# The gate of a noisy top-2 MoE kernel: its products accumulate in PSUM by quarters of a step and VectorE turns them, with no selection product

## The chip, the cores and the metric

The kernel runs on one core of a Trainium2 chip, in one launch, in fp32 and fp32r with a few bf16 tables. The metric is device time in microseconds. Three runs of the kernel before gave 718.95, 720.71 and 718.71 us, a median of 718.95 us.

## The reference, cut to what matters

A block-wise linear attention writes 3072 tokens of 512 features, and a mixture of 8 experts with a noisy top-2 gate follows on these tokens:

```python
# attention, per block of 64: out = ((q k^T) * Dmask) v + (q * lam_pow) kv_state
x = attn_out.transpose(0, 2, 1, 3).reshape(B * S, H * D)        # 3072 x 512
logits = x @ w_gate                                             # 512 x 8
noise_scale = np.log1p(np.exp(x @ w_noise))                     # 512 x 8
noisy_logits = logits + noise_scale * noise
top2 = np.argpartition(-noisy_logits, 2, axis=1)[:, :2]
# softmax over the two, then per expert e and choice k:
h = np.maximum(x[mask] @ w1[e], 0.0)
out[mask] += top2_w[mask, k, None] * (h @ w2[e])
```

The change concerns the two small products of the gate, `x @ w_gate` and `x @ w_noise`: 16 numbers per token out of 512 features.

## The kernel before, in words

**Two stages.** The first stage is the attention with the gate in it, up to about 140 us; the second is the experts. The order of every engine is written out by hand: the program is one long list, and each engine runs its own instructions in the order in which the list issues them.

**A step of the attention.** A step u is 256 tokens of all heads, two chunks `a` of 128; there are 12 steps. The loop `for t in range(NST)` (from L980) works on three steps at once. In iteration t TensorE turns the keys of step u = t + 1 (`trans_k`, L328), forms its key-value sums (`kv`, L419), turns its queries (`trans_q`, L344), does the product with the values of step t (`intra` and `inter`, L384), turns the output of step t - 1 into token rows (`store_x`, L450), does the gate's products of step t - 1 (`products`, L438), the scores of step u (`scores`, L372) and half of `inter`, and then the gate's selection of step t - 1 (`logits`, L466).

**The gate's products.** `wgn` holds gate and noise weights side by side, 16 columns and 16 zeros, for each of four blocks `d` of 128 features. `products` runs four matmuls, one per `d`, each over the 256 tokens of the step, into four groups of 32 partitions of the PSUM tile `pR`: the four partial sums stand below one another. ScalarE copies them to SBUF as `xp` (L440). `logits` multiplies `xp`, 128 tokens at a time, with the 0/1 matrix `sel` (made once by VectorE in `make_sel`, L256 to L259). This adds the four partial sums and puts the tokens on the partitions, into the PSUM tile `pL`. Each fp32 matmul stands in the trace as two records.

**PSUM tiles that are shared.** `pR` is one buffer, used in turn by `products`, by the second half of `kv` (a = 1) and by others. `pS` has four buffers: in an iteration `scores` takes all four, VectorE frees them with the masked copy `at` (L375, four instructions), and the next `trans_k` (three buffers) and `kv` (one) take them again.

**The routing.** The tokens are routed in three groups of 8 chunks (`GB`). After a group's last logits, VectorE runs `gate` (some 60 small instructions, beginning with a copy of the logits out of PSUM, L476), counts, and lists of tokens per expert tile. These jobs are Python generators; `advance(n)` issues about n us worth of them at two places of each iteration: after `trans_q` (`FILLS`, 3.4) and at its end (`FILL`, 2.0). A job that yields without a number counts 0.21. GpSimd computes the two softmax weights of a group, and `store_w` (L550) writes them with one DMA into the token rows in DRAM, on SP's queue.

**The end of the attention.** In the last iteration TensorE also turns the first gathered token rows (`trans_rows`, L874). Behind the loop come the first expert's first products (`mm1`, L895), the last step's products, `store_w(1)`, the last `store_x`, and the remaining list jobs. Then the attention's SBUF pools are closed, and the hidden tile `ht` takes their place: its first write, the ReLU of L901 on ScalarE, waits until all that used that memory is done, the DMA of the last `store_x` (L454) out of `xc` among it. VectorE's L905 forms the low part of `ht` and frees the PSUM buffer. The order of SP's queue there is: six DMAs of zeros into the output (L965), `store_w(1)`, the two of `store_x`, seventeen of zeros.

**Places.** A list entry is a token number, made by the one-hot matmuls of `enlist` from two parts, a chunk and a row in it (`tokb`, `rowf`, L621 to L648).

Of the kernel before, what the change touches and what calls it, by code (L numbers as in the profile page):

```python
# [59 lines left out]
HOT = 2 * (128 + NTL + NV * NTL)  # L60
NST = NCH // 2
NW = NC // 2
MAXOV = 40
ARENA = 1304
MAXT = 24
OPUS = 0.21
FILL, SPLIT, FILLS = 2.0, 1.2, 3.4
# [25 lines left out]
def sub(ap, offset, dims):  # L93
    return bass.AP(tensor=ap.tensor, offset=ap.offset + offset, ap=dims)
# [31 lines left out]
def kernel(  # L126
# [90 lines left out]
    def mask(s, h, c):  # L217
# [22 lines left out]
    iotar = consts.tile([128, TS], BF, name="iotar")  # L240
    nc.gpsimd.iota(iotar, pattern=[[1, TS]], base=0, channel_multiplier=0, allow_small_or_imprecise_dtypes=True)
    rowf = consts.tile([128, 1], FT, name="rowf")
    nc.gpsimd.iota(rowf, pattern=[[0, 1]], base=-TS, channel_multiplier=1, allow_small_or_imprecise_dtypes=True)
    tokb = consts.tile([128, NCH, NV], BF, name="tokb")
    nc.gpsimd.iota(tokb[:, :, 0], pattern=[[1, NCH]], base=-(BIG // TS), channel_multiplier=0,
                   allow_small_or_imprecise_dtypes=True)
    nc.gpsimd.iota(tokb[:, :, 1], pattern=[[0, NCH]], base=-TS, channel_multiplier=1,
                   allow_small_or_imprecise_dtypes=True)
    destf = consts.tile([128, 2, NCH], FT, name="destf")
    recs = consts.tile([128, NTL], I32, name="recs")  # L250
    sel = consts.tile([128, 2 * E], FT, name="sel")

    def make_sel():

        v = nc.vector
        v.tensor_scalar(sel, jp[:, 0:2 * E], 0.0, None, op0=OP.is_equal)  # L256
        for q in range(1, DB):
            v.tensor_scalar(sq4, jp[:, 0:2 * E], float(-32 * q), None, op0=OP.is_equal)
            v.tensor_add(sel, sel, sq4)  # L259

    sq4 = ac.tile([128, 2 * E], FT, name="sq4")

    class Arena:

        def __init__(self, n):
# [13 lines left out]
            return v  # L279

    arena = Arena(ARENA)
    for s, w in ((0, w_gate), (1, w_noise)):
        for d in range(2):
            for h in range(2):
                nc.gpsimd.dma_start(wgn[h * 64:(h + 1) * 64, d::2, s * E:(s + 1) * E],
                                  sub(w, (d * 128 + (h ^ d) * 64) * E, [[E, 64], [256 * E, DB // 2], [1, E]]))
# [29 lines left out]
    def half(i):  # L316
        return slice(i * 64, (i + 1) * 64)
# [115 lines left out]

    def products(u):

        p = psum.tile([128, 2, C], FT, name="pR")
        for d in range(DB):
            nc.tensor.matmul(p[d * 32:(d + 1) * 32], wgn[:, d, :], XO[u][:, :, d, :], start=True, stop=True)  # L438
        XP[u] = aw.tile([128, 2, C], FT, name="xp", bufs=1)
        nc.scalar.activation(XP[u], p, AF.Copy)  # L440

    XC = [ac.tile([128, DB, QW], FT, name=f"xc{i}") for i in range(3)]
    xturn = itertools.count()
# [12 lines left out]
    def logits(u):  # L456
        nonlocal pl
        for a in range(2):
            g = 2 * u + a
            b = max(i for i in range(NG) if GB[i] <= g)  # L460
            if not g:
                pl = psum.tile([128, 512], FT, name="pL")
            if g == GB[b]:
                PL[b] = pl[:, NV * NTL:][:, :GM * 2 * E].rearrange("p (c e) -> p c e", e=2 * E)
                PC[b] = pl[:, NV * NTL + GM * 2 * E:]
            nc.tensor.matmul(PL[b][:, g - GB[b], :], XP[u][:, a, :], sel, start=True, stop=True)  # L466


    def gate(b):
# [1 line left out]
        gs = GB[b + 1] - GB[b]  # L471
        sh = [128, gs, E]
        t = lambda sh, nm, dt=FT: arena.tile(sh, dt, name=nm)
        pl = PL[b]
        l2 = t([128, gs, 16], "l2")
        v.tensor_copy(l2, pl[:, :gs, :])  # L476
        yield
        zc = t(sh, "zc")
        v.tensor_scalar(zc, l2[:, :, 8:16], 87.0, -87.0, op0=OP.min, op1=OP.max)
        yield  # L480
# [65 lines left out]
        r["w"] = wd[:, 0]  # L546

    def store_w(b):
        rows = x_tok[GB[b] * C:GB[b + 1] * C, :].rearrange("(c p) w -> p c w", p=128)
        nc.sync.dma_start(rows[:, :, WAT:], RT[b].pop("w"))  # L550

    def count(b):
        gs = GB[b + 1] - GB[b]
# [63 lines left out]
    def loads(b, c, n, buf):  # L617

        _, hi, mv = hot(buf, n)
        mv = mv.rearrange("p k (w j) -> p k w j", w=NV)  # L620
        nc.vector.tensor_scalar(mv[:, :, 1, :], hi, rowf, None, op0=MULT)  # L621
        for i in range(n):
            k = slice(2 * i, 2 * i + 2)
            nc.vector.tensor_scalar(mv[:, k, 0, :], hi[:, k, :], float(GB[b] + c + i - BIG // TS), None, op0=MULT)

    found = consts.tile([128, NV, NTL], FT, name="found")

# [15 lines left out]
    def decode(s, out, n):  # L643

        v = nc.vector
        idf = rp.tile([128, n], FT, name=f"idf{n > 1}")
        v.scalar_tensor_tensor(idf, s[:, 0], float(TS), s[:, 1], op0=MULT, op1=ADD)
        v.tensor_scalar(out, idf, float(BIG + TS), None, op0=ADD)  # L648

    def read_lists(a, b):  # L650
# [31 lines left out]
        nc.vector.tensor_add(xo, xo, PO[0][0][half(g), g::2, :])  # L682
    kv(1)
    state(1)
    make_sel()
    inter(1, 1)

    def places(b):
# [292 lines left out]
    for t in range(NST):  # L981
# [16 lines left out]
        if not t:  # L998
            pass
        elif u < NST:  # L1000
            advance(FILLS)
        else:
            store_x(t - 1)
            products(t - 1)
            for j in range(PARTS0[0]):
                trans_rows(0, j)
            logits(t - 1)
            advance(FILLS)
        if t:
            intra(t)  # L1010
# [29 lines left out]
        if t >= NST - 2:  # L1040
            zero_out(3)
        if t == 2:
            nc.sync.dma_start(nz, sub(noise, 0, [[E, 128], [128 * E, NCH], [1, E]]))
    assert got
    finish(1)
    head = [mm1(0, 0, PARTS0[0], 0)]
# [280 lines left out]
```

## Time and profile before

| | |
|---|---|
| median of three runs | 718.95 us |
| span of the profiled execution, first to last instruction | 716.8 us |
| TensorE busy | 698.8 us, 97% |
| VectorE busy | 398.3 us, 56% |
| ScalarE busy | 223.3 us, 31% |
| GpSimd busy | 361.8 us, 50% |
| mean granted TensorE clock | 0.994 of full speed |
| largest share of the chain that ended last | TensorE, 89% |

The table says that TensorE is the engine to look at, and that it has hardly any idle time. It does not say what a microsecond taken from TensorE in one stage is worth: VectorE's 56% is a mean, and in the attention, where the gate's jobs run beside the masks, its share is far higher. So the stage of the change has to be read by itself, step by step. The profiled execution's own time is taken as its span; the median lies 2.15 us above it.

### The profile page before, as it was taken

The page shows a single profiled execution, that of the slowest core. Times are in us where ns is not written, and L with a number is a line of the kernel's source. Part 1 is how long each engine was busy: PE and PEld are TensorE (multiplying, and loading weights), DVE is VectorE, ACT ScalarE, POOL GpSimd, SP SyncE. Part 2 cuts the span into 40 slices and gives each one's busy share as a digit, 9 for nine tenths or more (in the row PEclk, how much of TensorE's full clock was granted, in tenths as well). Part 3 has the DMA queues.
Part 4 walks back from the last instruction along what each step waited for, and adds up shares of the span by engine and source line. Part 5 has one row for each costly group of instructions (what it writes and reads, how often), then busy time and mean ns, then how long its engine had stood idle before and what let it go on. Part 6 is the DMA issues. An engine that isn't in the chain of part 4 may idle for free.

```text
span 716.8 us, 15851 instructions
## 1 busy us (share of the span) xinstructions
PE 698.8 (97%) x6014; PEld 600.4 (84%) x6014; DVE 398.3 (56%) x1044; ACT 223.3 (31%) x382; POOL 361.8 (50%) x505
## 2 busy tenths in 40 slices
PE   7899999999999999999999999999999999999994
PEld 5888888889898898988888888888888898888883
DVE  4755899879355546743674367337624662565210
ACT  2255545542143312332233214222322242223100
POOL 4411342313453865687768567836773768321221
PEclk9999999999999999999999999999999999999998
DMA  9998986580645725273627352735452554330110
GB/s 203 263 230 245 251 232 203 188 305 25 180 131 168 207 56 179 82 185 87 183 93 176 85 186 84 176 88 161 116 154 79 170 143 122 104 116 30 51 51 32
DMA packets 94192, 104.32 MB, mean 146 GB/s; under 512 B 41234, under 2 KB 66844, under 8 KB 94112
## 3 DMA queue, kind: packets, MB, share of 16 engines
q1 hardware_dynamic: 79456, 65.73, 34.0%
q0 software_dynamic: 13552, 37.00, 17.0%
q10 hardware_dynamic: 1104, 0.53, 0.5%
q8 instruction: 49, 0.80, 0.5%
q14 instruction: 31, 0.25, 0.1%
HBM read 78.28 MB, written 26.12 MB: 146 GB/s over the span
## 4 chain that ended last, share of the span: by engine, by line
PE 89%; issue 4%; DMA 2%; POOL 1%; DVE 1%; ACTq 0%; SPq 0%; ACT 0%; POOLq 0%
PE pS L895 37%; PE pKV L933 16%; PE pO L933 16%; PE pO L384 3%; PE pS L372 3%; PE pS L328 2%; PE pS L450 2%; PE pO L938 2%; PE pS L419 2%; PE pS L344 1%; PE pKV L384 1%; PE pKV L938 1%; DMA Mk<-powd 1%; PE pR L438 1%; PE pS L874 1%
## 5 line engine op out<-in xcount | busy, mean ns | idle before, releaser
L839 POOL DMA_INDIRECT xg<-x_tok,recq x147 | 161.0, 1095 | 45.6 <-issue 40.0
L895 PE MATMUL pS<-xth,w1h 128*128 128x512 f32 (+3 forms) x544 | 181.4, 333 | 0.9 <-DVE ht L905 0.9
L895 PE MATMUL pS<-xth,w1l 128*128 128x512 f32 (+3 forms) x544 | 180.5, 332 | 0.0
L895 PE MATMUL pS<-xtl,w1h 128*128 128x512 f32 (+3 forms) x544 | 180.5, 332 | 0.0
L905 DVE SCALAR_TENSOR_TENSOR ht<-pS,ht 128x256 fp32r<-128x256 f32 (+3 forms) x176 | 75.8, 454 | 123.1 <-ACT ht L901 120.7
L933 PE MATMUL pKV<-w2h,ht 128*128 128x512 f32 x384 | 122.6, 390 | 0.0
L933 PE MATMUL pO<-w2h,ht 128*128 128x512 f32 x384 | 122.4, 390 | 0.0
L952 POOL DMA_INDIRECT out_dram<-ot,rec x46 | 60.7, 1319 | 121.0 <-DVE ot L945 110.8
L901 ACT ACTIVATE ht<-pS 128x512 fp32r<-128x512 f32 (+3 forms) x136 | 65.2, 483 | 173.2 <-PE pS L895 167.7
L895 PEld LDWEIGHTS pS<-xth,w1h 128*128 128x128 f32 x544 | 102.7, 189 | 10.4 <-DVE ht L905 1.1
L895 PEld LDWEIGHTS pS<-xth,w1l 128*128 128x128 f32 x544 | 102.7, 189 | 8.8
L895 PEld LDWEIGHTS pS<-xtl,w1h 128*128 128x128 f32 x544 | 102.7, 189 | 8.8
L933 PEld LDWEIGHTS pO<-w2h,ht 128*128 128x128 f32 x384 | 72.1, 188 | 14.9
L933 PEld LDWEIGHTS pKV<-w2h,ht 128*128 128x128 f32 x384 | 72.1, 188 | 14.9
L866 ACT ACTIVATE xth<-turned 128x512 fp32r<-128x512 f32 (+1 forms) x39 | 23.7, 607 | 167.5 <-DVE turned L864 167.5
L933 PE MATMUL pKV<-w2l,ht 128*128 128x512 f32 x192 | 74.9, 390 | 0.0
L933 PE MATMUL pO<-w2l,ht 128*128 128x512 f32 x192 | 74.8, 390 | 0.0
L360 POOL TENSOR_TENSOR kd<-kt,Mk 128x512 f32<-128x512 f32 x24 | 24.8, 1051 | 73.4 <-PE pR L419 51.6
L917 POOL DMA_INDIRECT pv<-out_dram,rec x46 | 47.0, 1021 | 14.2 <-issue 12.0
L375 DVE TENSOR_TENSOR at<-pS,Mk 128x512 f32<-128x512 f32 x48 | 29.9, 683 | 23.0 <-PE pS L372 18.5
L808 DVE TENSOR_TENSOR w2l<-wst,w2h 128x1024 fp32r<-128x1024 f32 (+1 forms) x33 | 39.2, 1191 | 6.1 <-ACT w2h L807 5.6
L933 PEld LDWEIGHTS pKV<-w2l,ht 128*128 128x128 f32 x192 | 36.1, 188 | 7.4
(241 smaller groups left out, 941.5 us busy)
## 6 DMA issues: line engine op xcount, KB each, us to landing
wst<-in_moe_w_dram SPq DMA_DIRECT2D x36, 512.0 KB, 4.2
wst<-in_moe_w_dram SPq DMA_DIRECT2D x96, 128.0 KB, 3.7
x_tok<-xc SPq DMA_DIRECT2D x24, 272.0 KB, 4.7
kt<-in_k_dram SPq DMA_DIRECT2D x12, 512.0 KB, 5.2
qt<-in_q_dram SPq DMA_DIRECT2D x24, 256.0 KB, 5.2
vt<-in_v_dram SPq DMA_DIRECT2D x12, 512.0 KB, 5.7
out_dram<-zero SPq DMA_DIRECT2D x24, 256.0 KB, 3.6
xg<-x_tok,recq POOLq DMA_INDIRECT x147, 2.8
```

Of the source, the lines that this page charges most:

```text
L360: nc.gpsimd.tensor_mul(kd[:, :, s], kt[:, :, s], mask(s, slice(0, HP), slice(C - 1, C)).to_broadcast([128, HP, 2, D]))
L375: nc.vector.tensor_mul(at[:, s], ps[s], mask(s, slice(2 * r, 2 * r + 2), slice(0, C)))
L384: nc.tensor.matmul(PO[u][a][half(g), hp, :], lhs, rhs, start=n == 1, stop=n == (8 if not (u % NW or a) else 12 if u else 10))
L808: nc.vector.tensor_tensor(lo[:, r], st[:, r], hi[:, r].bitcast(FT), op=SUB)
L839: nc.gpsimd.indirect_dma_start(out=XG[t][:, g * QW:(g + 1) * QW], out_offset=None, in_=x_tok.rearrange("t (q w) -> (t q) w", w=QW), in_off ...
L866: nc.scalar.activation(hi, raw, AF.Copy)
L895: nc.tensor.matmul(p, W1[a][d][:, fs], xt(b, cs)[:, d], start=(d == 0 and i == 0), stop=(d == DB - 1 and i == 2))
L901: nc.scalar.activation(ht(e, 0, f, cs), p, AF.Relu)
L905: nc.vector.scalar_tensor_tensor(ht(e, 1, f, c), p[:, r], 0.0, ht(e, 0, f, c).bitcast(FT), op0=OP.max, op1=SUB)
L917: nc.gpsimd.indirect_dma_start(out=PV[t][:size(e, t), :], out_offset=None, in_=out, in_offset=bass.IndirectOffsetOnAxis(ap=REC[e, t], axis=0),
L933: nc.tensor.matmul(p, ht(e, a, f, cs), W2[b][f // 2][:, f % 2, :], start=(i == 0), stop=(i == len(terms) - 1))
L952: st = nc.gpsimd.indirect_dma_start(out=out, out_offset=bass.IndirectOffsetOnAxis(ap=REC[e, t], axis=0), in_=o, in_offset=None, bounds_che ...
```

## The change

The products go by quarters of 64 tokens. For each block `d` of features and each quarter `j` there is one matmul of 64 columns, into the group `j` of 32 partitions of `pR`, and the four blocks `d` add up there in PSUM (`start` on the first, `stop` on the last). So 16 matmuls stand where 4 were, with as many columns in all. VectorE then turns the 128 x 64 tile in blocks of 32 x 32 straight out of PSUM (`transpose`), which puts the tokens on the partitions. ScalarE's copy `xp`, the two selection matmuls of a step, `sel` with `make_sel`, and the copy at the head of `gate` are gone. `pR` is now held until VectorE has turned it.

A token now stands on another partition: token 64 j + 32 g + i of a step is on partition 32 j + i, in column group g. So the noise and the weights are moved by eight DMAs each instead of one (128 descriptors of 32 bytes each for the weights), the place tables are built from more pieces, and the decoding of list entries uses 32 instead of 128. In the last iteration `logits` stands ahead of `trans_rows`, with one dummy matmul behind (`keep_warm(1)`).

```diff
-ARENA = 1304
+ARENA = 1432
-    nc.gpsimd.iota(rowf, pattern=[[0, 1]], base=-TS, channel_multiplier=1, allow_small_or_imprecise_dtypes=True)
-    nc.gpsimd.iota(tokb[:, :, 0], pattern=[[1, NCH]], base=-(BIG // TS), channel_multiplier=0,
...
+    for j in range(4):
+        for o, n in ((rowf, 1), (tokb[:, :, 1], NCH)):
+            nc.gpsimd.iota(o[j * 32:(j + 1) * 32], pattern=[[0, n]], base=64 * j - TS, channel_multiplier=1,
...
-        p = psum.tile([128, 2, C], FT, name="pR")
+        p = XP[u] = psum.tile([128, 2, 32], FT, name="pR")
         for d in range(DB):
-            nc.tensor.matmul(p[d * 32:(d + 1) * 32], wgn[:, d, :], XO[u][:, :, d, :], start=True, stop=True)
-        XP[u] = aw.tile([128, 2, C], FT, name="xp", bufs=1)
-        nc.scalar.activation(XP[u], p, AF.Copy)
+            for j in range(4):
+                nc.tensor.matmul(p[j * 32:(j + 1) * 32], wgn[:, d, :], XO[u][:, j // 2, d, half(j % 2)],
+                                 start=d == 0, stop=d == DB - 1)
...
-                PL[b] = pl[:, NV * NTL:][:, :GM * 2 * E].rearrange("p (c e) -> p c e", e=2 * E)
-                PC[b] = pl[:, NV * NTL + GM * 2 * E:]
-            nc.tensor.matmul(PL[b][:, g - GB[b], :], XP[u][:, a, :], sel, start=True, stop=True)
+                PL[b] = lg1 if b == 1 else arena.tile([128, GM, 32], FT, name="l2")
+                PC[b] = pl[:, NV * NTL:]
+            if not a:
+                nc.vector.transpose(PL[b][:, g - GB[b]:][:, :2, :].rearrange("p g e -> p (g e)"),
+                                    XP[u].rearrange("p g r -> p (g r)"))
...
-        l2 = t([128, gs, 16], "l2")
-        v.tensor_copy(l2, pl[:, :gs, :])
-        yield
+        l2 = PL[b][:, :gs, :]
...
-        rows = x_tok[GB[b] * C:GB[b + 1] * C, :].rearrange("(c p) w -> p c w", p=128)
-        nc.sync.dma_start(rows[:, :, WAT:], RT[b].pop("w"))
+        w = RT[b].pop("w")
+        for j in range(4):
+            for g in range(2):
+                rows = x_tok[GB[b] * C + 64 * j + 32 * g:, :]
+                nc.sync.dma_start(sub(rows, WAT, [[XW, 32], [2 * C * XW, w.shape[1] // 2], [1, E]]),
+                                  w[j * 32:(j + 1) * 32, g::2, :])
...
-    make_sel()
...
             products(t - 1)
+            logits(t - 1)
             for j in range(PARTS0[0]):
                 trans_rows(0, j)
-            logits(t - 1)
+            keep_warm(1)
             advance(FILLS)
...
-            nc.sync.dma_start(nz, sub(noise, 0, [[E, 128], [128 * E, NCH], [1, E]]))
+            for j in range(4):
+                for g in range(2):
+                    nc.sync.dma_start(nz[j * 32:(j + 1) * 32, g::2, :],
+                                      sub(noise, (64 * j + 32 * g) * E, [[E, 32], [2 * C * E, NST], [1, E]]))
```

TensorE's order in iteration 4, from `store_x` to the next `trans_k` (`xo` is the attention's output of a step, `qTs` the scaled queries, `S` a state; `pO` and `pKV` take the output). Before:

```order
L450 MATMUL pS<-identf,xo 128x128 x8
L438 MATMUL pR<-xo,wgn 32x256 x4
L372 MATMUL pS<-qT,kT 64x128 x32
L384 MATMUL pKV<-qTs,S_150 64x128
L384 MATMUL pO<-qTs,S_149 64x128
...
L466 MATMUL pL<-sel,xp 128x16 x2
L328 MATMUL pS<-identf,kt 128x128 x12
```

With the change:

```order
L441 MATMUL pS<-identf,xo 128x128 x8
L430 MATMUL pR<-xo,wgn 32x64 x16
L363 MATMUL pS<-qT,kT 64x128 x32
L375 MATMUL pKV<-qTs,S_150 64x128
L375 MATMUL pO<-qTs,S_149 64x128
...
L319 MATMUL pS<-identf,kt 128x128 x12
```

The selection is gone, so `trans_k` follows on `inter`, and the products have four times as many matmuls of a quarter of the columns.

VectorE's order from the masked copy of iteration 4 to that of iteration 5, where the first group's gate begins (`arena` is the gate's scratch memory; L476 is the copy out of PSUM; the constants' lines L101 to L118 are a polynomial). Before:

```order
L375 TENSOR_TENSOR at<-pS,Mk 128x512 x4
L476 COPY arena<-pL 128x128
L479 TENSOR_SCALAR arena<-arena 128x64
...
L500 TENSOR_TENSOR arena<-arena 128x64
L505 MAX arena<-arena 128x8
L375 TENSOR_TENSOR at<-pS,Mk 128x512 x4
L505 MAX arena<-arena 128x8 x7
```

With the change (`lg` takes the second group's logits):

```order
L366 TENSOR_TENSOR at<-pS,Mk 128x512 x4
L458 STREAM_TRANSPOSE arena<-pR 128x64
L469 TENSOR_SCALAR arena<-arena 128x64
...
L490 TENSOR_TENSOR arena<-arena 128x64
L495 MAX arena<-arena 128x8 x3
L366 TENSOR_TENSOR at<-pS,Mk 128x512 x4
L458 STREAM_TRANSPOSE lg_173<-pR 128x64
L495 MAX arena<-arena 128x8 x5
```

The transpose has the place of the copy, it comes in every iteration and not once a group, and two more instructions of the gate (L495) now stand ahead of the masked copy.

SP's order at the end of the attention, around `store_w(1)`. Before:

```order
L965 DMA out_dram<-zero 128x512 x3
L550 DMA x_tok<-arena 128x8x8
L454 DMA x_tok<-xc_183 128x544
L454 DMA x_tok<-xc_184 128x544
L965 DMA out_dram<-zero 128x512 x17
```

With the change:

```order
L959 DMA out_dram<-zero 128x512 x3
L543 DMA x_tok<-arena 32x4x8 x8
L445 DMA x_tok<-xc_188 128x544
L445 DMA x_tok<-xc_189 128x544
L959 DMA out_dram<-zero 128x512 x17
```

The last two stores of token rows now stand behind eight DMAs of weights instead of one.

## Rows read from the trace of the kernel before

**Rows 1.** The page's first line.

```profile
span 716.8 us, 15851 instructions
```

**Rows 2.** Busy time by stretch: PE, PEld, DVE, ACT, POOL, then clock, DMA share, GB/s.

```profile
108.00:126.00 18.00, 17.96 (x404) 15.23 (x402) 16.42 (x58) 10.11 (x19) 4.27 (x4) 1.00 0.65 200
```

**Rows 3.** Chain that ended last, attention: start us, us, engine, tile, line, records.

```profile
67.03 0.57 PE pR L438 x8
67.60 1.91 PE pS L372 x64
69.94 0.55 PE pL L466 x4
70.49 1.36 PE pS L328 x12
...
77.90 1.91 PE pS L372 x64
...
80.78 1.36 PE pS L328 x12
...
83.28 1.02 PE pS L344 x8
...
92.89 1.08 PE pS L419 x32
...
109.40 1.91 PE pS L372 x64
...
120.26 1.91 PE pS L372 x64
...
123.19 1.85 PE pS L328 x12
```

**Rows 4.** Timeline of PE: start us, us, engine, line, operation, out<-in, count.

```profile
91.19 0.34 PE L561 MATMUL pL<-arena,ones 128*128 128x8 bf16 x8
```

**Rows 5.** Timeline of DVE, iterations 4, 5, 8 and 9.

```profile
68.67 2.48 DVE L375 TENSOR_TENSOR at<-pS,Mk 128x512 f32<-128x512 f32 x4 [3.43 <-PE pS L372]
71.07 0.28 DVE L476 COPY arena<-pL 128x128 f32<-128x128 f32 x1
...
79.55 2.46 DVE L375 TENSOR_TENSOR at<-pS,Mk 128x512 f32<-128x512 f32 x4
81.93 0.56 DVE L505 MAX8 arena<-arena 128x8 f32<-128x8 f32 x7
...
110.47 2.48 DVE L375 TENSOR_TENSOR at<-pS,Mk 128x512 f32<-128x512 f32 x4 [0.72 <-PE pS L372]
...
122.46 2.46 DVE L375 TENSOR_TENSOR at<-pS,Mk 128x512 f32<-128x512 f32 x4
```

**Rows 6.** Line L864, VectorE's transposes later on: ns min/median/max, then forms.

```profile
L864 DVE STREAM_TRANSPOSE turned<-xg x39: 298/702/712, 268.1 to 641.6; 128x512 f32<-128x512 f32 x36, 128x128 f32<-128x128 f32 x3
```

**Rows 7.** Timeline of SP's queue at the end of the attention.

```profile
141.97 0.38 SPq L550 DMA_DIRECT2D x_tok<-arena  x1
143.09 1.05 SPq L454 DMA_DIRECT2D x_tok<-xc  x2
144.19 11.35 SPq L965 DMA_DIRECT2D out_dram<-zero  x17
```

**Rows 8.** Timeline of ACT and PE there.

```profile
146.31 0.66 ACT L901 ACTIVATE ht<-pS 128x256 fp32r<-128x256 f32 x2 [2.76 <-DMA x_tok<-xc]
...
146.85 1.58 ACT L807 ACTIVATE w2h<-wst 128x1024 fp32r<-128x1024 f32 x2
...
148.99 0.39 PE L895 MATMUL pS<-xth,w1h 128*128 128x256 f32 x1 [0.92 <-DVE ht L905]
```

**Rows 9.** Timeline of DVE there.

```profile
148.51 0.76 DVE L905 SCALAR_TENSOR_TENSOR ht<-pS,ht 128x256 fp32r<-128x256 f32 x2
149.18 1.81 DVE L808 TENSOR_TENSOR w2l<-wst,w2h 128x1024 fp32r<-128x1024 f32 x2
150.91 0.42 DVE L905 SCALAR_TENSOR_TENSOR ht<-pS,ht 128x256 fp32r<-128x256 f32 x1
```

More of the change, by code (lines that the diff above doesn't have):

```diff
@@ L62 @@
 NW = NC // 2
+QT32 = 32
 MAXOV = 40
-ARENA = 1304
+ARENA = 1432
 MAXT = 24
@@ L242 @@
     rowf = consts.tile([128, 1], FT, name="rowf")
-    nc.gpsimd.iota(rowf, pattern=[[0, 1]], base=-TS, channel_multiplier=1, allow_small_or_imprecise_dtypes=True)
     tokb = consts.tile([128, NCH, NV], BF, name="tokb")
-    nc.gpsimd.iota(tokb[:, :, 0], pattern=[[1, NCH]], base=-(BIG // TS), channel_multiplier=0,
-                   allow_small_or_imprecise_dtypes=True)
-    nc.gpsimd.iota(tokb[:, :, 1], pattern=[[0, NCH]], base=-TS, channel_multiplier=1,
-                   allow_small_or_imprecise_dtypes=True)
+    nc.gpsimd.iota(tokb[:, :, 0].rearrange("p (u g) -> p u g", g=2), pattern=[[8, NST], [1, 2]], base=-(BIG // QT32),
+                   channel_multiplier=0, allow_small_or_imprecise_dtypes=True)
+    for j in range(4):
+        for o, n in ((rowf, 1), (tokb[:, :, 1], NCH)):
+            nc.gpsimd.iota(o[j * 32:(j + 1) * 32], pattern=[[0, n]], base=64 * j - TS, channel_multiplier=1,
+                           allow_small_or_imprecise_dtypes=True)
     destf = consts.tile([128, 2, NCH], FT, name="destf")
     recs = consts.tile([128, NTL], I32, name="recs")
[L251 to L261, printed above, removed]
     class Arena:
@@ L281 @@
     arena = Arena(ARENA)
+    lg1 = ac.tile([128, GM, 32], FT, name="lg1")
     for s, w in ((0, w_gate), (1, w_noise)):
@@ L473, in gate @@
         t = lambda sh, nm, dt=FT: arena.tile(sh, dt, name=nm)
-        pl = PL[b]
-        l2 = t([128, gs, 16], "l2")
-        v.tensor_copy(l2, pl[:, :gs, :])
-        yield
+        l2 = PL[b][:, :gs, :]
         zc = t(sh, "zc")
@@ L623, in loads @@
             k = slice(2 * i, 2 * i + 2)
-            nc.vector.tensor_scalar(mv[:, k, 0, :], hi[:, k, :], float(GB[b] + c + i - BIG // TS), None, op0=MULT)
+            nc.vector.tensor_scalar(mv[:, k, 0, :], hi[:, k, :], float((GB[b] + c + i) // 2 * 8 + (c + i) % 2 - BIG // QT32), None,
+                                    op0=MULT)
     found = consts.tile([128, NV, NTL], FT, name="found")
@@ L646, in decode @@
         idf = rp.tile([128, n], FT, name=f"idf{n > 1}")
-        v.scalar_tensor_tensor(idf, s[:, 0], float(TS), s[:, 1], op0=MULT, op1=ADD)
+        v.scalar_tensor_tensor(idf, s[:, 0], float(QT32), s[:, 1], op0=MULT, op1=ADD)
         v.tensor_scalar(out, idf, float(BIG + TS), None, op0=ADD)
```

## The prediction

> **What bounds the kernel now.** I read the page first, then the busy time by stretch, the chain of waits over the attention, and the timelines of VectorE, SP and ScalarE where that chain leaves TensorE. The sum is made against the span of the profiled execution, 716.8 us [rows 1]; the median of the runs, 718.95 us, lies 2.15 above it, and I add the same 2.15 at the end. In the attention TensorE is busy 17.96 of 18 us at a granted clock of 1.00, but VectorE is not idle there either: 16.42 of 18 [rows 2]. So TensorE sets the pace with VectorE close behind. A step, from one scores group to the next, takes 77.90 - 67.60 = 10.30 us [rows 3]. The gate has two pieces in it: the products (L438, 0.57 us) and the selection (L466, 0.55 us), both on the chain [rows 3].
>
> **The selection's end.** Its 0.55 us do not all go. A full-array transpose costs 1.36 / 12 = 0.113 us (L328 behind the selection); L344 behind 64x64 work takes 1.02 for eight, where 8 x 0.113 would be 0.91 [rows 3]. The change of tile shape thus costs 0.11. The selection pays it today, as the first full-array work behind `inter`; with it gone `trans_k` pays it. Gain: 0.55 - 0.11 = 0.44 us a step.
>
> **The products.** They go from 8 records to 32, with the same columns. The scores are 64 records of 128 columns over four 64x64 tiles that run beside each other: 16 records a tile in 1.91 us, 0.119 each, 0.93 ns a column [rows 3]. Today a group of 32 partitions has 2 records of 256 columns, 0.48 us of 0.57; changed, 8 of 64 columns, again 0.48. What 24 more records cost is shown by `kv`: its full form, 64 records, runs from 80.78 + 1.36 = 82.14 to 83.28, 1.14 us; its half form, 32 records on two of the four tiles, takes 1.08 [rows 3]. 32 more records beside the others: 0.06 us. I take 0 for the products. From below the bound is 0.48 (-0.09 a step). From above, the tiny full-array matmuls of the counting run one behind the other, eight in 0.34 us, 0.043 each [rows 4]; 32 of these are 1.36 us (+0.79 a step). I stay with `kv`, which has small tiles, short records and PSUM accumulation too.
>
> One rule speaks against that. The Trainium skill, in "TensorEngine Tiling (Array Packing)", section "Instruction Overhead", gives every matmul some 60 cycles of overhead and advises against making a dimension smaller that is already small. By an estimate from this page, 24 more records at 25 ns would be 0.6 us a step, and the time 721.6 us; the `kv` pair above measures a tenth of that, so the trace does not agree where tiles run side by side, and I keep it as a reason for the second rival.
>
> **VectorE's transpose.** 128 x 64 out of PSUM stands nowhere in the trace. VectorE's transposes from SBUF take 0.298 us for 128 columns and 0.70 for 512 [rows 6], 1.05 ns a column, so 0.23 for 64; the copy of 128 x 128 out of PSUM, 0.28 [rows 5], bounds it from above, though a source in PSUM could add to that. I take 0.25. It stands behind the fourth masked copy and holds `pR` until its end; queued behind it are the gate's jobs, and who waits is the second half of `kv`. Where the masked copy is on time it starts 68.67 - 67.60 = 1.07 us after the scores and ends at 1.07 + 2.48 = 3.55, the transpose at 3.80 [rows 3, 5]. `kv` will be reached at 1.91 + 0.43 (`inter`) + 0.11 + 1.36 = 3.81. That just fits: no wait in iterations 1, 2, 3, 6 and 7, a gain of 5 x 0.44 = 2.20 us.
>
> **Where VectorE is late, the gain is lost.** In iterations 5 and 9 the masked copy starts with no idle time before it [rows 5]: VectorE comes straight from the gate's polynomials. Then TensorE's saved time only makes it wait longer for `pS` and `pR`.
>
> Iterations 4 and 5: VectorE needs 79.55 - 68.67 = 10.88 us from copy to copy [rows 5]. The change takes 0.30 from it (L476), adds 0.25 (a transpose) and 2 x 0.08 (two of L505 more ahead of the copy, 0.56 for seven): 10.99. So, counted from the scores of iteration 4, the copy of iteration 5 starts at 1.07 + 10.99 = 12.06, ends at 14.54, the transpose at 14.79, and `kv` starts there; today it starts at 82.14 - 67.60 = 14.54. Two steps together lose 0.25 us.
>
> Iterations 8 and 9: 122.46 - 110.47 = 11.99 becomes 12.10; from the scores of iteration 8 the copy starts at 1.07 + 12.10 = 13.17 and ends at 15.65, and `kv` (here the half form, without `pR`) follows at 15.70; today it starts at 123.19 + 1.85 - 109.40 = 15.64 [rows 3, 5]. A loss of 0.06.
>
> Up to the scores of iteration 10 this makes 2.20 - 0.25 - 0.06 = 1.89 us.
>
> **The end of the attention.** From there to 148.99 TensorE's own savings count little, since it waits there anyway (0.92 us, for L905 [rows 8]); this also covers the selections of the last steps and the dummy matmul. What decides is when `ht` can be written. ScalarE's L901 waits until 146.31 for the last store of token rows [rows 8], whose two issues end at 143.09 + 1.05 = 144.14, behind the one DMA of weights at 141.97 [rows 7]. Now eight go ahead. One takes 0.38 us of SP, one of the large ones behind 11.35 / 17 = 0.67 [rows 7]. I take 0.42, near the small one: 8 x 0.42 = 3.4. Two transposes of VectorE delay the weights by some 0.2: first issue 142.2, last one done at 145.6, stores at 146.65, 2.5 later than today. L901 then starts at 148.8. Its first half is done at 149.15, L905 of it at 149.55 (0.38), and TensorE goes on there instead of at 148.99: +0.55. For the third part ScalarE has its two L807 (1.58) ahead, VectorE two L808 (1.81) that need these; its L905, today at 150.91, comes at about 152.3 [rows 8, 9]. TensorE wants that buffer after two more parts of 1.5 us, at 152.55, and gets it at 152.75. In all +0.75 us.
>
> **Costed at nothing.** Six more iotas on GpSimd in the first 3 us (it then waits for the mask's DMA), the noise's eight DMAs (loads there run three steps ahead), `store_w(0)` (the same), `store_w(2)` (SP has nothing else to issue for some 7 us then), ScalarE's freed 0.4 us a step, `make_sel`. What TensorE does behind 155 us is unchanged and moves as a block.
>
> **Sum.** -1.89 + 0.75 = -1.14: span 715.7, time 717.8 us.
>
> **Rivals.**
>
> First, VectorE makes room: the gate's jobs may start from an earlier point or run shorter without L476, so that nothing is lost in iterations 4, 5, 8 and 9. Then nine steps gain 9 x 0.44 = 3.96, less 0.75: 715.7 us. For it: VectorE has 0.72 us of idle time before the copy of iteration 8 [rows 5]. Against it: in 5 and 9 there is none, and each step gets a transpose more. With the products at their lower bound (9 x 0.09) and no delay at the end this reaches 714.2.
>
> Second, slower: the 32 short records of the products do not run beside each other, or are issued at a fixed price each. It decides from (0.57 + 0.44) / 32 = 0.032 us a record on. At the 0.043 of [rows 4], twelve steps lose 12 x (0.79 - 0.44) = 4.2, with the end 723.9 us; one group after the other (32 x 64 columns x 0.93 ns = 1.9 us) would be worse still. For it: rows 4. Against it: `kv` and the products of today, whose four groups overlap.
>
> Third, the queue: each small DMA holds SP for 0.67, as the zeros do. Then the stores come 2 us later still and TensorE goes on some 2 us later: 719.8 us, no change again, with the other sign.
>
> **How the numbers follow.** What a measurement of this kernel tells from no change is about 0.3%, 2.2 us: from 716.8 to 721.1. My forecast, 717.8, has 0.52; the first rival 0.27, the second 0.10, the third 0.11. Faster takes the first rival and the lower edge of the forecast, 0.33; slower the second and a little of the third, 0.11; the rest, 0.56, is no change. The range goes from 714.2 (first rival at its bounds) to 721.0, which leaves most of the second rival out. The likeliest case's own range is 716.6 to 719.2.
>
> **What would show it.** In the profile of the changed kernel: the products' group of 16 matmuls takes 0.55 to 0.65 us from its start to the scores' start; a step of iterations 1 to 3 is 9.8 to 9.9 us long instead of 10.3; VectorE's transpose takes 0.2 to 0.3 us; the first `kv` record of iteration 6 (step 7) waits for that transpose; SP spends some 3.4 us on eight issues before the last store, and L901 waits for this store, with a TensorE gap of over 1 us behind it. The prediction is wrong if the products take over 0.8 us, if iterations 5 and 9 gain like the others, or if ScalarE's L901 starts no later than today.

## The result: slower by 0.7%

Six runs of the changed kernel took 722.55 to 727.88 us, median 723.52; six of the kernel before on the same chip 718.71 to 720.71, median 718.92. The ratio is 1.0067, with a 95% interval of 1.0046 to 1.0087. Forecast were 717.8 us and "no change". The profiled execution has a span of 722.9 us, 716.8 before [rows 1]. The profiled execution of the changed kernel took 724.7 us, 1.2 above its median, so the account below has some 6 us to explain where the medians differ by 4.6. The first four experiments below ran on a disturbed chip, where the kernel before took 739.5 us and TensorE's granted clock was half for 7 to 14 us between 259 and 282 us, so of these only the ratio and the attention are used.

The chain of waits in the changed kernel's attention (start us, us, engine, tile, line, records; L430 are the products, L363 the scores, L319 `trans_k`, L410 `kv`, L375 `intra` and `inter`) answers to [rows 3]:

```profile
37.29 0.58 PE pR L430 x32
37.88 1.91 PE pS L363 x64
...
47.79 0.58 PE pR L430 x32
48.38 1.91 PE pS L363 x64
...
68.08 0.17 PE pR L430
68.26 0.65 issue
68.91 0.65 PE pR L430 x31
69.56 1.91 PE pS L363 x64
71.46 0.10 PE pKV L375 x2
...
71.90 1.46 PE pS L319 x12
...
73.62 0.18 issue
73.80 0.33 PE pR L410 x4
...
77.87 1.29 issue
79.16 0.27 PE pO L375
```

The products take 0.58 us for 32 records, as forecast, and no selection stands between `inter` and `trans_k`. New is "issue": TensorE stands still and waits for nothing that the profile names, in the middle of the products, of `kv` and of `intra`. In the view of waits of the attention (waiting tile and line, what it waited for, us in total, times, longest) the kernel before has none of these rows:

```profile
PE pR L410 <- issue: 1.9, 2, 1.7
PE pR L430 <- issue: 1.5, 2, 0.9
PE pS L319 <- DVE at L366: 1.5, 1, 1.5
PE pO L375 <- issue: 1.3, 1, 1.3
PE pS L335 <- ACT qT L338: 0.8, 1, 0.8
...
PE pKV L375 <- issue: 0.6, 1, 0.6
PE pS L410 <- issue: 0.4, 1, 0.4
```

**What the gaps are.** Count TensorE's records, matmuls and weight loads together, from the first. The six gaps of 0.39 us and more stand at records (counted from 0) 449, 705, 1473, 2753, 3265 and 5569: 449 and 449 plus 1, 4, 9, 11 and 20 times 256; a seventh, of 0.18 us, stands at 3009, 10 times 256 on. On the DMA queue q8, of the kind "instruction", the first 165 us have 27 packets of 16 KB, about one for each 256 records. In the trace, the packet before the gap of 1.29 us starts at 76.62 and ends at 77.60; TensorE goes on at 79.16, 1.56 us later. For the other five it is 1.44 to 1.52 us. So I read the gaps as instruction blocks that come late; that a packet belongs to a given block is inferred from this count. The wait that the view puts down to `qT` begins at such a record too (4801, 17 times 256 on), 1.35 us behind a packet's end, and in `a_nokd` below the profile names no releaser for a gap at the same record; so it may be supply as well. The queues while that packet was moved (packets, MB, share of 16 engines):

```profile
q1 hardware_dynamic: 437, 0.15, 57.3%
q8 instruction: 1, 0.02, 6.2%
```

TensorE had entered the block before at 73.80, so the packet started 2.81 us later. Over the blocks entered between 30 and 130 us, a packet starts 2.17 us after TensorE enters the block before and takes 1.10; with the 1.5 us this makes 4.8 us. The kernel before needs 1.62 + 1.16 + 1.5 = 4.3, and a block lasts it 5.27 us. No block there starts less than 1.50 us behind its packet's end, and two start within 0.01 us of that: it had no gap that the view of waits counts, and hardly a margin. A step before has 509 records and loads on the mean of nine, the changed one 40 more. In the run where no block comes late (`a_neither`, below) a block of the changed kernel lasts 4.8 us on the mean, no longer than the 4.8 that a packet needs: no margin is left for a packet that is later than the mean. The Trainium skill, in "Runtime: NRT & Kernel Launch", section "Instruction fetch mechanics", says that a sequencer fetches its instructions in blocks of 16 KiB, 256 instructions, through a DMA queue of its own, and that this is mostly hidden, since the engine takes them up more slowly than they come. The blocks agree with the trace; that they are hidden does not, with 3.4 us of gaps in nine steps.

**VectorE's part.** Two of its gate instructions around 108 us, and the same two in a run without GpSimd's scaling of the keys (`a_nokd`, below):

```profile
107.36 0.99 DVE L615 TENSOR_SCALAR hb<-hb,rowf 128x224 bf16<-128x224 bf16 x1
108.27 1.16 DVE L618 TENSOR_SCALAR hb<-hb 128x112 bf16<-128x112 bf16 x2
```

```profile
106.15 0.28 DVE L618 TENSOR_SCALAR hb<-hb,rowf 128x224 bf16<-128x224 bf16 x1
106.35 0.28 DVE L621 TENSOR_SCALAR hb<-hb 128x112 bf16<-128x112 bf16 x2
```

What stands beside them on GpSimd, whose scaling (`kd`) starts when `kv` has ended:

```profile
107.23 2.06 POOL L351 TENSOR_TENSOR kd<-kt,Mk 128x512 f32<-128x512 f32 x2 [4.21 <-PE pR L410]
```

Behind 30 us, six such instructions take about 1 us instead of 0.2 to 0.3 (at 75, 87, 88, 107, 108 and 119 us), and L642 behind the last one too; in the kernel before it is one, at 83.6 us. The states (L422), which read PSUM, take 0.28 beside the scaling as always. The Trainium skill ("SBUF — State Buffer", section "Who interferes with whom") has the rule: a VectorE instruction with two inputs in SBUF contends with a GpSimd instruction that reads SBUF, a copy, cast or tensor_scalar in a fast mode contends with GpSimd, and whichever comes first blocks the other for its whole instruction. The rows agree: 0.99 us beside the scaling, 0.28 without it. So the masked copy of iteration 8 starts late, with no idle time before it, and that of iteration 9 later still, answering to [rows 5]:

```profile
114.13 2.48 DVE L366 TENSOR_TENSOR at<-pS,Mk 128x512 f32<-128x512 f32 x4
...
127.68 2.46 DVE L366 TENSOR_TENSOR at<-pS,Mk 128x512 f32<-128x512 f32 x4
```

**The end.** SP's eight DMAs of weights, the last two stores and TensorE's return, answering to [rows 7 to 9]; piece of the chain, changed kernel:

```profile
147.08 0.33 SPq L543
...
147.45 0.68 SPq L543
...
148.18 0.43 SPq L543
...
151.57 0.38 SPq L445
...
152.00 2.52 DMA out_dram<-zero
154.51 0.42 DVE ht L899
...
154.98 1.10 PE pS L889 x7
```

The piece of the zeros' DMA is what VectorE's L899 waited for last. ScalarE's first write of `ht` ahead of it waits for the last store, by the view of waits:

```profile
ACT ht L895 <- DMA x_tok<-xc: 5.0, 1, 5.0
```

Before, this wait was 2.76 us [rows 8]. L895 starts 17.76 us behind the scores of step 11, L901 before 15.25: 2.5 later, as forecast. TensorE waits 1.87 us for `ht` instead of 0.92.

**The account.** "Scores" is the first record of that step's scores, "end" the way from the scores of step 11 to the first expert's second product.

| kernel | start to scores 2 | scores 2 to 11 | TensorE's waits in it | end |
|---|---|---|---|---|
| before | 36.16 | 94.91 | none | 24.16 |
| changed | 37.81 | 98.51 | supply 3.4, masked copy 1.5, `qT` 0.8 | 24.97 |

The sum of the differences is 1.65 + 3.60 + 0.81 = 6.06 us; behind it both kernels need 561.6 us. In the first stretch the changed kernel has two gaps, 0.56 and 1.68. But this 1.65 is not shown to be the change's: in the profiles of the changed kernel and its variants the scores of step 2 start between 34.9 and 38.3 us, in those of the kernel before and its variants between 35.7 and 37.8. The other two make 4.4 us, near the 4.6 of the medians.

In the second stretch the waits are 5.7. A gap shows less than the whole stop: TensorE's last record before it lasts 0.22 to 0.27 us, and the next would have started within that time. Counted from start to start, less what is usual between two such records, the stops come to some 7.4 us. Without them the stretch would be some 3.8 us shorter than before, nine steps at 0.42. The forecast of 1.89 is not the number to hold against this, as VectorE's lateness is part of it.

### The profile page after: what moved, and what is told of

Its sections match the earlier page's. It is cut to its first block, busy times and chain, and to the rows that moved or that the text cites. A ratio compares the mean times of both kernels' runs of the same rounds, so it can differ in the third digit from the quotient of the medians.

```text
span 722.9 us, 16349 instructions
## 1 busy us (share of the span) xinstructions
PE 699.5 (97%) x6255; PEld 602.7 (83%) x6255; DVE 403.0 (56%) x1046; ACT 219.2 (30%) x370; POOL 361.4 (50%) x511
## 4 chain that ended last, share of the span: by engine, by line
PE 86%; issue 5%; DVE 5%; POOL 1%; DMA 1%; SPq 1%; ACT 0%; POOLq 0%; DVEq 0%; ACTq 0%
PE pS L889 37%; PE pKV L927 16%; PE pO L927 16%; PE pS L363 2%; PE pO L375 2%; PE pS L319 2%; PE pO L932 2%; PE pS L335 1%; PE pS L410 1%; PE pS L441 1%; PE pKV L375 1%; DVE at L366 1%; PE pKV L932 1%; POOL out_dram L946 1%; PE pS L868 1%
## 5 line engine op out<-in xcount | busy, mean ns | idle before, releaser
L899 DVE SCALAR_TENSOR_TENSOR ht<-pS,ht 128x256 fp32r<-128x256 f32 (+3 forms) x176 | 75.8, 454 | 123.5 <-ACT ht L895 120.2
L895 ACT ACTIVATE ht<-pS 128x512 fp32r<-128x512 f32 (+3 forms) x136 | 65.2, 483 | 174.0 <-PE pS L889 166.4
L927 PEld LDWEIGHTS pO<-w2l,ht 128*128 128x128 f32 x192 | 36.0, 188 | 7.3
```

The costliest lines, as they stand in the source:

```text
L895: nc.scalar.activation(ht(e, 0, f, cs), p, AF.Relu)
L899: nc.vector.scalar_tensor_tensor(ht(e, 1, f, c), p[:, r], 0.0, ht(e, 0, f, c).bitcast(FT), op0=OP.max, op1=SUB)
L927: nc.tensor.matmul(p, ht(e, a, f, cs), W2[b][f // 2][:, f % 2, :], start=(i == 0), stop=(i == len(terms) - 1))
```

## The experiments

Theories: **supply** (late instruction blocks) and **held** (gate instructions beside GpSimd's scaling); rivals are the price of a record, `pR`, the DMAs. The first four runs are `a_four`, `b_split16`, `a_noq` and `b_noq`.

**Four matmuls again** (`a_four`).

```diff
-            for j in range(4):
-                nc.tensor.matmul(p[j * 32:(j + 1) * 32], wgn[:, d, :], XO[u][:, j // 2, d, half(j % 2)], ...)
+            nc.tensor.matmul(p[d * 32:(d + 1) * 32], wgn[:, d, :], XO[u][:, :, d, :], start=True, stop=True)
```

> The changed kernel, with the gate's products as four matmuls of 256 columns again (no accumulation; VectorE turns the first 64 columns of each group, so the logits hold one block of features and the tokens of one quarter only). TensorE gets 16 records and weight loads a step instead of 64, with the same columns; VectorE's transpose, the token places, the DMAs and the order of all engines stay those of the changed kernel. Theory (instruction supply): TensorE ran dry at the end of blocks of 256 records, because the next 16 KB block of instructions came late; with 48 fewer a step it comes in time: no TensorE gap without a releaser, 717 to 720.5 us. Rival (VectorE's transposes, pR held longer, the eight DMAs, the places): nothing of that is touched, 722.5 to 724.5 us.

Ratio 0.9984 (0.9929 to 1.0038). Scores 2 to 11: 96.97 us, with two gaps, 2.2 and 0.5, and 1.1 for the masked copy; the steps without a gap took 9.87. It agrees with supply in part: fewer gaps, but the gap of 2.2 followed a packet that started 4.89 us after TensorE had entered the block before. One late packet is enough, with few records too.

**Cut in place** (`b_split16`): the kernel before with four matmuls for one, block by block.

```diff
+            for j in range(4):
+                nc.tensor.matmul(p[d * 32:(d + 1) * 32, j // 2, half(j % 2)], wgn[:, d, :], XO[u][:, j // 2, d, half(j % 2)], ...)
```

> The kernel before, with each of the four products matmuls cut into four of 64 columns, into the same places of the same tile (16 matmuls, the selection kept): 48 more records and weight loads a step, nothing else. Theory (instruction supply): TensorE gaps without a releaser appear in the attention, each at a multiple of 256 records and some 1.5 us behind the end of a 16 KB instruction packet, 2 to 5 us in all: 721 to 724 us. Rival (the records cost no more than their columns, and the loss is VectorE's or the DMAs'): 719 to 719.7 us. Rival (a fixed price a record of 0.02 us or more): the products' group is over 1 us long, 724 us.

Ratio 1.0102 (0.9991 to 1.0213). The steps took 11.04 us, since four matmuls in a row went to one group of partitions:

```profile
60.03 1.32 PE pR L439 x32
```

Compare 0.58 for the same 32 records where each goes to the next group. So the run says little on the supply (gaps of 0.9, 1.3 and 0.3 us), but much on the order.

**The next group each time** (`b_rot16`): the same with `for j` outside and `for d` inside; **32 matmuls** of 32 columns (`b_rot32`).

> The kernel before, with the products as 16 matmuls of 64 columns into the same places, in an order in which each goes to the next group of 32 partitions: 24 more TensorE records and 24 more weight loads a step, everything else as before. Products 0.55 to 0.65 us long, since four groups run beside each other. Theory (instruction supply): gaps without a releaser, each at the first record of a block of 256 and some 1.5 us behind the end of a 16 KB instruction packet, 2 to 5 us in all up to the end of the attention; from the packets' waits measured so far and 4.8 us a block instead of 5.2, some 2 us more than in the kernel before on the same chip. Rival (the changed kernel lost its time to VectorE, pR or the DMAs): no more than 0.7 us, twelve steps at 0.06.

> The kernel before, with the products as 32 matmuls of 32 columns, each going to the next group of 32 partitions: 56 more TensorE records and 56 more weight loads a step than before (the run with 16 matmuls had 24 and 24 more). Theory (instruction supply): a block of 256 now lasts 4.4 us of work instead of 5.2; from the packets' waits measured so far the gaps at block starts add up to 8.6 us over the attention, where the kernel before has 2 by the same account: the attention ends some 6 us later than before, and the gaps stand at the first record of a block, 1.4 to 1.6 us behind the end of a 16 KB packet. Rival (a price per short record): the products' group itself grows by as much as the steps do, and no gap without a releaser stands outside it.

`b_rot16`: ratio 1.0038 (1.0018 to 1.0058), 722.2 against 719.77 us; the attention ends 3.4 us later. `b_rot32`: 1.0234 (1.0206 to 1.0263), and 17.6 us later. The chain of the latter (its products are 64 records, here 50 of them):

```profile
42.52 1.26 issue
...
47.94 0.65 issue
...
50.27 0.69 PE pR L440 x50
...
52.41 1.65 issue
```

The products of `b_rot16` take 0.58 us, and its gaps between scores 2 and 11 come to 2.3 us; those of `b_rot32` to 10.1, all at starts of blocks (449 + 256 n, within a record), 1.29 to 1.54 us behind a packet's end. By the count from start to start, 3.7 of the 3.75 us by which this stretch of `b_rot16` is longer than before (98.66 against 94.91) are lost at starts of blocks. In `b_rot32` it is 13.9 us longer; its products take 0.69 us instead of 0.57, which makes 1.1 of these, so a price of the short records is the small part. Layout, VectorE's work and DMAs are those of the kernel before, and still a packet of `b_rot16` waits 2.16 us on the mean, so that the change's small DMAs are not needed for it. So the supply alone makes a kernel with more records slower, and most gaps stand in the scores, the transposes and `kv`, not in the short records.

**Without the queries' loads** (`a_noq`, `b_noq`).

```diff
+            if u >= 3:
+                QT[u] = QT[u - 2]
+                return
```

> The changed kernel without the query loads of steps 3 to 11 (the queries of steps 1 and 2 are used again): some 0.5 MB of small packets a step less on the DMA queue, all instructions of the engines as before. Theory (instruction supply, with the packet waiting behind data): the instruction packets start within 1 us of the request, the gaps vanish in the attention, and the time is that of the kernel before with the same cut, plus or minus 1.5 us: 716 to 719 us. Rival (VectorE, pR, the eight DMAs at the end): still 4 us above the kernel before with the same cut.

> The kernel before without the query loads of steps 3 to 11, the control of the run with the changed kernel. Both theories: within 1.5 us of the kernel before, 717.5 to 719.5 us, since its instruction blocks came in time anyway.

Ratios 0.9999 (0.9938 to 1.0061) and 0.9964 (0.9916 to 1.0012). A packet's mean wait fell only from 2.17 to 1.30 us, and 3.2 us of gaps stayed in `a_noq`: supply's expectation failed there, since this load was not the whole queue.

**Without any of these loads** (`a_noload`, `b_noload`): the same edit for keys and values too.

> The changed kernel without the loads of queries, keys and values from step 3 on (those of steps 0 to 2 are used again); the weights' loads and the token rows' stores stay. Theory (instruction supply, packets behind data): between 40 and 130 us the packets start within 1 us of a block's entry in most cases, and the gaps without a releaser there fall from 3 to 5 us to under 1.5. What is left above the kernel before with the same cut is VectorE's lateness (its instructions beside GpSimd's scaling) and the end. Rival (the packets wait for something else, or the gaps come from TensorE itself): the gaps stay at 3 us or more.

> The kernel before with the same cut, as the control: steps of 10.3 us, no gaps at block starts between 40 and 130 us, and packets that start within 1 us of a block's entry.

One run each. The mean wait is 0.50 and 0.52 us, and past 30 us no gap is left in either. The steps of `a_noload` up to the scores of step 6 take 9.86 to 9.89 us, the forecast's 9.86. But then TensorE waits for VectorE; VectorE's timeline (iterations 4 and 5) and TensorE's one wait between scores 2 and 11:

```profile
68.42 2.48 DVE L370 TENSOR_TENSOR at<-pS,Mk 128x512 f32<-128x512 f32 x4 [3.44 <-PE pS L367]
...
72.52 2.32 DVE L102 SCALAR_TENSOR_TENSOR arena<-arena 128x64 f32<-128x64 f32 x3
...
80.88 2.46 DVE L370 TENSOR_TENSOR at<-pS,Mk 128x512 f32<-128x512 f32 x4
```

```profile
PE pS L323 <- DVE at L370: 4.3, 2, 2.3
```

From copy to copy 12.46 us, where the forecast had 10.99. The three L102, 0.73 elsewhere, take 2.32. A second cost follows: behind the first of these two waits the granted clock was 0.50 from 82.6 to 86.0 us, and `trans_k`, elsewhere 1.46 us, takes 2.31:

```profile
81.61 2.31 PE L323 MATMUL pS<-identf,kt 128*128 128x128 f32 x12 [2.05 <-DVE at L370]
```

By an estimate, 3.4 us at half the clock cost 1.7 us. Span 724.3 against 716.9: no better than the changed kernel; its end is 2.9 us longer as well (27.03 against 24.15), with the clock at half once more (last section).

**Without the scaling** (`a_nokd`), and **without both** (`a_neither`).

```diff
+        if u >= 3:
+            KD[u] = KD[2]
+            return
```

> The changed kernel without GpSimd's scaling of the keys from step 3 on (the scaled keys of step 2 are used again). Theory of a second part of the loss: VectorE's SBUF instructions take some 1 us instead of 0.2 to 0.3 while GpSimd's scaling runs; these five vanish, VectorE is no longer late for the masked copy of iteration 9, and the attention ends 1.5 to 2.5 us earlier. Rival (instruction supply alone): VectorE's lateness is covered by TensorE's gaps, and the attention ends less than 0.5 us earlier.

> The changed kernel without the loads of queries, keys and values from step 3 on (those of steps 0 to 2 are used again) and without GpSimd's scaling of the keys from step 3 on (that of step 2 is used again): both causes taken away at once. If late instruction blocks and VectorE's held instructions are the whole loss, no TensorE gap without a releaser stands between 40 and 130 us, VectorE's masked copies of iterations 4 and 5 lie 10.9 to 11.0 us apart and those of 8 and 9 some 11.9 to 12.1, and the stretch from the scores of step 2 to those of step 11 is 92.5 to 94 us, shorter than the 94.5 of the kernel before with the loads cut. Rival (a third cause): 95.5 us or more.

`a_nokd` routes its tokens otherwise and takes longer in the second stage (772.02 us, ratio 1.0734), so only its attention counts: no held instruction behind 30 us, and 4.5 us of gaps left between scores 2 and 11. It ends 3.2 us earlier than the changed kernel's, but 2.6 of these lie ahead of the scores of step 2, a start that varies by as much without the cut; between scores 2 and 11 the gain is 0.6, nearer to what the rival expected (under 0.5) than to the theory (1.5 to 2.5). In `a_neither` (719.53 us, one run, beside 719.19 of the kernel before) the masked copies are those of the forecast:

```profile
66.93 2.48 DVE L373 TENSOR_TENSOR at<-pS,Mk 128x512 f32<-128x512 f32 x4 [3.44 <-PE pS L370]
77.82 2.46 DVE L373 TENSOR_TENSOR at<-pS,Mk 128x512 f32<-128x512 f32 x4
...
107.99 2.48 DVE L373 TENSOR_TENSOR at<-pS,Mk 128x512 f32<-128x512 f32 x4 [0.56 <-PE pS L370]
119.86 2.47 DVE L373 TENSOR_TENSOR at<-pS,Mk 128x512 f32<-128x512 f32 x4
```

10.89 and 11.87 us, forecast 10.99 and 12.10. The four cases together:

| changed kernel | scores 2 to 11 | waits in it |
|---|---|---|
| as it is | 98.51 | supply 3.4, copy 1.5, `qT` 0.8 |
| loads cut | 97.58 | copy 4.3; half clock for 3.4 us |
| scaling cut | 97.88 | supply 4.5 |
| both cut | 92.27 | copy 1.4 |
| kernel before, loads cut | 94.49 | none |

Either cause by itself costs nearly as much as both: a gap of TensorE hides VectorE's lateness, and the other way round. Of the 5.3 us between "loads cut" and "both cut", 2.9 are the longer wait for the copy and some 1.7 the clock that fell behind it. With both gone the change gains 2.2 us there. In the changed kernel's own stretch the granted clock is full, and no third cause is needed. Each row is one profile; the second one of the changed kernel (`after_again`, below) has 100.90. The kernel before with both cut was not run; it waits nowhere in this stretch as it is.

**Moved work** (`a_fill`), **a wait for the scaling** (`a_kdwait`), and the changed kernel again.

```diff
-FILL, SPLIT, FILLS = 2.0, 1.2, 3.4
+FILL, SPLIT, FILLS = 1.2, 1.2, 4.2
```

```diff
             state(u)
+            nc.gpsimd.tensor_copy(spacer, SA[u, 1][0:1, 0, 0:1])
             kdecay(t + 2)
```

> The changed kernel with less of the gate's work at the end of an iteration and more behind the queries (1.2 and 4.2 us worth instead of 2.0 and 3.4): VectorE reaches the states before GpSimd's scaling of the keys starts, and the gate's instructions that took 1 us beside the scaling (at 75, 107 to 109 and 118 to 120 us) stand behind the states. Theory of the second part of the loss: these instructions take 0.2 to 0.3 us again, and the attention ends 1.5 to 3 us earlier than in the changed kernel: 720.5 to 722 us. Rival (TensorE's gaps cover it): 723 to 724 us.

> The changed kernel, with a one-element copy ahead of GpSimd's scaling of the keys that waits for VectorE's first new state: the scaling then runs beside the states and the scaled queries, which it did not hold up, instead of beside the gate's instructions. The output stays the reference's. Theory of the held instructions: they take 0.2 to 0.3 us, TensorE waits for the masked copy less than 0.5 us in all, the gaps of the instruction supply stay at 4 to 5 us, and the time is 719.5 to 721.5 us. Rival (the gaps of the supply cover it): 722.5 to 724 us.

> The changed kernel once more, as the control on the same chip: 722.5 to 724 us, with gaps of 3 to 6 us at block starts, at other blocks than in its first profile where the packets' waits differ.

`a_fill` is worse, 1.012 (1.0092 to 1.0148): no instruction was held behind 30 us, but the gate's work comes later at the end, where TensorE waits 3.0 us for `ht` instead of 1.9. `a_kdwait` took 723.49 us, 1.0063 (1.0045 to 1.0082) of the kernel before; `after_again` 725.94, 1.0071 (1.0049 to 1.0093). The time for which instructions were held, over the shortest of their kind, fell from 4.8 us in `after_again` to 1.9 (0.8 of each at 21 us), but the gaps stayed (5.8 and 6.6 us between scores 2 and 11), and the times do not separate the two: the expectation of 721.5 at most failed. In `after_again` the gaps stand at other blocks, as the packets' waits differ from run to run.

**The end term** (`a_late_w`, and with the wait `a_both`).

```diff
-    store_w(1)
     store_x(NST - 1)
+    store_w(1)
```

> The changed kernel with the eight DMAs of the second group's weights behind the last two stores of token rows on SP's queue. Theory of the end term: ScalarE's first write of ht waits for a store that is now issued some 3 us earlier, TensorE's wait before the second part of the first expert goes from 1.9 to about 1 us, and the time falls by 0.7 us. Rival (the wait is hidden, or the gather of rows becomes the bound): no change.

> The same, and the eight DMAs of the second group's weights behind the last two stores of token rows. By the end term 0.7 us less than without: 718.8 to 720.8 us, about the kernel before. Rival: no difference between the two.

`a_late_w`: 1.0047 (1.0033 to 1.006), 723.48 us. TensorE's wait for `ht` is 0.9 us again, and the end 23.96 us instead of 24.97, but the time shows no 0.7: its attention has supply gaps of 4.3 us, and the spread hides the term. `a_both`: 1.0051 (1.0033 to 1.0069), 722.71 us, end 23.95. The best version found of the changed kernel is still slower than the kernel before.

**Logits at once** (`b_direct`): tokens stationary, four matmuls of 16 columns for each chunk.

```diff
+                nc.tensor.matmul(PL[b][:, g - GB[b], :], XO[u][:, a, d, :], wgn[:, d, :2 * E], start=d == 0, stop=d == DB - 1)
```

> The kernel before, with the tokens as the stationary operand: for each chunk of 128 tokens four matmuls of 16 columns add up over the blocks of features, and the logits stand with the tokens on the partitions at once; no copy of ScalarE, no selection, no transpose, places and DMAs as before. 16 full-array records a step instead of 8 and 4. At 0.043 us each (the counting's 128x8 bf16) they take 0.7 us instead of 0.57 + 0.55, a gain of 0.3 a step with the change of tile shape, 716 to 718 us by the instruction supply's account (8 more records and loads a step). At 0.113 each (a transpose) they take 1.8 us and the time is 725 to 728.

Ratio 1.0165 (1.0142 to 1.0187), 730.91 us: above even the upper case of 725 to 728. Its end is 2.4 us longer than before too (26.59), which was not taken apart. A step's 16 records, from TensorE's timeline:

```profile
57.23 1.86 PE L445 MATMUL pL<-wgn,xo 128*128 128x16 f32 x16
```

## Why the prediction was wrong

Two steps of the working failed, both in the attention: "I take 0 for the products", and VectorE's 10.99 and 12.10 us from copy to copy. None of the three signs of being wrong appeared: the products took 0.58 us (two of the twelve were longer, by a gap inside them), iterations 5 and 9 did not gain, and `ht` was written later.

- **What bounds the kernel.** TensorE and VectorE were named. A third thing was just as near its limit and has no term in the sum: TensorE's instruction queue. It showed in the trace of before, in packets that ended 1.50 us ahead of their block.
- **The products at 0.** Right in their own time, 0.57 to 0.58 us; `kv` was the right comparison, and the 0.6 us a step behind the second rival did not show. The failed step is that a record's price was sought in its duration alone. 24 more of them, with their weight loads, cost 0.01 us beside their neighbours and some 0.4 us a step through the supply: 3.7 us in the nine steps of `b_rot16`, 2.3 of them seen as gaps.
- **The selection's end, 0.44 us a step.** Right: steps of 9.86 to 9.89 where neither cause is at work, 10.29 or 10.30 before.
- **VectorE's transpose, 0.25.** Right: 0.24 (L458). One sign is missing: `kv` of iteration 6 does not wait for it. In `a_neither`, where the copies run as forecast, TensorE waits 0.47 us for the copy, ahead of `trans_k`.
- **VectorE late, 10.99 and 12.10 us.** The second failed step. Right with loads and scaling cut (10.89, 11.87). With the scaling 12.46 in `a_noload` and, in the changed kernel, 127.68 - 114.13 = 13.55. The sum took every instruction at its duration in the old place. But the change brought `kv`, and with it GpSimd's scaling, forward to where VectorE is still at the gate. In the kernel before the scaling of iteration 4 started only 0.05 us after the last gate instruction ahead of the states had started.
- **The end, 0.75.** Right in size, 24.16 to 24.97, and in its way: with the stores ahead of the eight issues (`a_late_w`) it is 23.96 again. The eight issues take 3.9 us instead of 3.4.
- **The sum.** The stretch of the steps was forecast to gain 1.89; it lost 3.60. With both causes cut it gains 2.2, so the other terms of the stretch hold.
- **The rivals.** The second, slower, named almost the time (723.9), by luck: its mechanism is refuted, with 0.018 us a record, not 0.043. The first, that VectorE makes room, was the opposite of what happened. The third had 0.67 us for each small DMA; it is 0.43.

## What to carry to other kernels

Count instructions, not only their time: where an engine runs through 256 records in about 5 us while the DMA engines are full, its instruction blocks can come late, and the profile then shows idle time that nothing explains, at equal distances in the program. When a change moves one engine forward, look at which pairs of instructions now run side by side, since a VectorE instruction on SBUF can wait out a whole one of GpSimd. Where two causes overlap, taking away one shows almost nothing; take away both before you drop either. And look at the granted clock in a run that takes one away: a new wait of TensorE can bring it down (here 2.05 us of wait and, by the estimate above, 1.7 more at half the clock).

## What the runs showed of the hardware that was not expected

- Four matmuls in a row into one group of 32 partitions run one after the other: 32 records in 1.32 us, against 0.58 where each goes to the next group.
- With a wait of TensorE of 2.2 to 3.0 us for `ht` (`a_noq`, `a_noload`, `a_neither`, `a_fill`) the granted clock was half for 3.4 us; behind waits of 0.9 to 1.9 us there it stayed full. The length of the wait alone does not decide it: behind 2.05 us at 81.61 in `a_noload` the clock fell, behind 2.27 at 127.29 there and 2.23 at 76.58 in `a_four` it did not. In `a_neither` (us, PE, PEld, DVE, ACT, POOL, clock, DMA share, GB/s):

```profile
145.00:147.90 2.90, 0.23 (x2) 0.02 (x1) 1.05 (x5) 0.93 (x3) 0.00 (x0) 1.00 1.02 378
148.30:151.70 3.40, 3.40 (x18) 3.40 (x17) 3.09 (x6) 3.40 (x9) 0.00 (x0) 0.50 1.02 381
152.00:155.00 3.00, 3.00 (x28) 3.00 (x27) 1.46 (x5) 1.90 (x5) 0.00 (x0) 1.00 1.03 384
```

That makes its end 27.30 us, though it has the shortest steps: a gain in front of a longer wait was given back at half the clock.
